# Windowed attention and a two-stage MoE layer on one core: a generator weave replaced by a planned program, with Q, K and x turned by DMA

## The chip, the core and the metric

The kernel runs on one core of a Trainium2 chip. The metric is the device time of one execution in microseconds. TensorE (PE) does the matmuls, with PEld its weight loads; VectorE (DVE), ScalarE (ACT) and GpSimd (POOL) do the elementwise work; SyncE (SP) issues transfers. PSUM holds what PE writes, and only DVE and ACT move it from there to SBUF.

## The reference

For 8 batches of 8 heads with 576 positions of 64 channels, attention over a causal window of 64 positions:

```python
scores = scale * np.matmul(q, k.transpose(0, 1, 3, 2))
mask = (rel >= 0) & (rel < window)          # rel = pos[:, None] - pos[None, :], window = 64
attn = softmax(np.where(mask, scores, -1e9))
attn_out = np.matmul(attn, v)
```

The heads of a position are joined to a row of 512, which gives x with 4608 rows, and then comes a layer with weights 512 x 2048 and 2048 x 512:

```python
h = x @ w_in
g = h * np.clip(h + 3.0, 0.0, 6.0) / 6.0
out = g @ w_out
```

All inputs and the output are float32.

## The kernel before

Matmuls take bf16 and add up in float32. The contraction runs over partitions, so Q, K and x are needed with channels on the partitions, and they arrive with positions there. Attention works on a pair of heads (group g, 4 per batch), since two heads of 64 channels fill 128 partitions; positions are cut into 5 blocks of 128.

The steps of a group, as generators in `attention` (line 170):

- `tq` (173): six PE transposes of Q (line 178) into a PSUM tile `tr`, copied to `QT` by DVE (187), then the same for K, copied by ACT (189). The casts to bf16 before it are `cast_batch` (149): DVE and ACT in batch 0, POOL later.
- `scores` (192): matmuls K x Q in two parts, key blocks 0 and 1, then 2, 3 and 4 (201); exp on ACT (208, 214); one multiply by the 0/1 mask on DVE (219).
- `pv` (224): 18 matmuls P x V (231, 236). V carries a column of ones, so the sum of a row comes along; reciprocal and product on DVE (242, 245) give `opg`.
- `xt` (251): five PE transposes (255), copied to `xT` by ACT (260).

The MoE layer works on blocks of 512 rows of x, 9 of them. `s1(T)` (273) makes 16 chunks of 128 hidden channels, each of 4 matmuls of 512 columns (280), a RELU on ACT (285) and a min-and-multiply on DVE (286). `s2(T)` (291) makes 4 tiles of 128 rows, each of 16 matmuls of 512 columns (296), a copy on ACT (303) and a store (305).

What sets the order is the program order of these generators. `zipped` (308) takes turns between a chunk of `s1(T)` and a quarter tile of `s2(T - 1)`, and `weave` (319) puts pieces of the next batch's attention between them by a fixed ratio. PSUM is given out by purpose: one `tr`, one `st`, one `o`, two `hT`, one `acc`.

Loads of a batch (`load_batch`, 67) are issued on SP: Q and K with six positions on each of 96 partitions (runs of 1536 B), V in five blocks with a position on each partition (runs of 256 B per head). There is one staging buffer per tensor, so the load of the batch after waits for the casts. The weights come by POOL's own queue with a cast on the way (94, 101).

Of the kernel before, what the change touches and what calls it, by code (L numbers as in the profile page):

```python
# [14 lines left out]
MIN = mybir.AluOpType.min  # L15
ISGE = mybir.AluOpType.is_ge
PSUM = bass.MemoryType.PSUM

WINDOW = 64


@with_exitstack
def kernel(
# [18 lines left out]
    R = 6  # L42
    NP = S // R
    NFC = FF // P
    TB = 512
    NTB = NT // TB
    assert NTB * TB == NT and NP * R == S
    QW = P + WINDOW
    VW = D + 1
    scale = 1.0 / math.sqrt(D)  # L50

    consts = ctx.enter_context(tc.tile_pool(name="consts", bufs=1))
    stage = ctx.enter_context(tc.tile_pool(name="stage", bufs=1))
    nat = ctx.enter_context(tc.tile_pool(name="nat", bufs=2))
    small = ctx.enter_context(tc.tile_pool(name="small", bufs=4))
    opool = ctx.enter_context(tc.tile_pool(name="opool", bufs=2))
    gpool = ctx.enter_context(tc.tile_pool(name="gT", bufs=2))
    t1pool = ctx.enter_context(tc.tile_pool(name="t1", bufs=3))
    osbp = ctx.enter_context(tc.tile_pool(name="osb", bufs=3))
    ps_tr = ctx.enter_context(tc.tile_pool(name="ps_tr", bufs=1, space=PSUM))  # L60
    ps_st = ctx.enter_context(tc.tile_pool(name="ps_st", bufs=1, space=PSUM))
    ps_o = ctx.enter_context(tc.tile_pool(name="ps_o", bufs=1, space=PSUM))
    ps_h = ctx.enter_context(tc.tile_pool(name="ps_h", bufs=2, space=PSUM))
    ps_acc = ctx.enter_context(tc.tile_pool(name="ps_acc", bufs=1, space=PSUM))


    def load_batch(b, by_pair):
        qst = stage.tile([P, H, R * D], F32, name="qst", tag="qst")
        kst = stage.tile([P, H, R * D], F32, name="kst", tag="kst")
        vst = stage.tile([P, KB, H, D], F32, name="vst", tag="vst")  # L70
        step = 2 if by_pair else H
        for h0 in range(0, H, step):
            for dst, src in ((qst, q), (kst, k)):
                nc.sync.dma_start(
                    out=dst[:NP, h0 : h0 + step, :],
                    in_=src[b, h0 : h0 + step].rearrange("h (p j) d -> p h (j d)", j=R),
                )
        for kb in range(KB):
            s0 = kb * P
            ss = min(P, S - s0)  # L80
            nc.sync.dma_start(  # L81
                out=vst[:ss, kb, :, :],
                in_=v[b, :, s0 : s0 + ss, :].rearrange("h s d -> s h d"),
            )
        return qst, kst, vst

    stage0 = load_batch(0, True)


    win16 = consts.tile([P, NG, FF], BF16, name="win16")  # L90
    wout16 = consts.tile([P, NFC, DM], BF16, name="wout16")
    WC = FF // 4
    for i in range(4):
        nc.gpsimd.dma_start(
            out=win16[:, :, i * WC : (i + 1) * WC],
            in_=moe_w_in[:, i * WC : (i + 1) * WC].rearrange("(g p) f -> p g f", p=P),
        )

    def load_w_out():
        for i in range(0, NFC, 4):  # L100
            nc.gpsimd.dma_start(
                out=wout16[:, i : i + 4, :],
                in_=moe_w_out[i * P : (i + 4) * P, :].rearrange("(c p) j -> p c j", p=P),
            )


    ident32 = consts.tile([P, P], F32, name="ident32")
    make_identity(nc, ident32)
    ident = consts.tile([P, P], BF16, name="ident")
    nc.vector.tensor_copy(out=ident[:], in_=ident32[:])  # L110
    mask32 = consts.tile([P, QW], F32, name="mask32")
    nc.gpsimd.memset(mask32[:], 1.0)
    nc.gpsimd.affine_select(
        out=mask32[:], in_=mask32[:], pattern=[[1, QW]], compare_op=ISGE,
        fill=0.0, base=0, channel_multiplier=-1,
    )
    nc.gpsimd.affine_select(
        out=mask32[:], in_=mask32[:], pattern=[[-1, QW]], compare_op=ISGE,
        fill=0.0, base=WINDOW - 1, channel_multiplier=1,
    )  # L120
    mask = consts.tile([P, 2 * KB, QW], BF16, name="mask")
    nc.vector.tensor_copy(
        out=mask[:], in_=mask32[:].unsqueeze(1).to_broadcast([P, 2 * KB, QW])
    )
    half = consts.tile([P, 1], F32, name="half")
    nc.vector.memset(half[:], 0.5)


    NQT, NPT, NV = 3, 3, 2
    QT_ring, KT_ring, P_ring, V_ring = [], [], [], []  # L130
    for i in range(NQT):
        for ring, n in ((QT_ring, "QT"), (KT_ring, "KT")):
            t = consts.tile([P, SP], BF16, name=f"{n}{i}")
            nc.vector.memset(t[:, S:SP], 0.0)
            ring.append(t)
    for i in range(NPT):
        t = consts.tile([P, 2, KB, 2 * P], BF16, name=f"pT{i}")
        nc.gpsimd.memset(t[:], 0.0)
        P_ring.append(t)
    for i in range(NV):  # L140
        t = consts.tile([P, KB, H, VW], BF16, name=f"V{i}")
        nc.gpsimd.memset(t[:, :, :, D:VW], 1.0)
        nc.gpsimd.memset(t[D:P, KB - 1, :, 0:D], 0.0)
        V_ring.append(t)

    xT = consts.tile([P, NG, NT], BF16, name="xT")


    def cast_batch(b, st, first):
        qst, kst, vst = st  # L150
        qn = nat.tile([P, R, H, D], BF16, name="qn")
        kn = nat.tile([P, R, H, D], BF16, name="kn")
        V = V_ring[b % NV]
        step = 2 if first else H
        for h0 in range(0, H, step):
            for i, (n, s) in enumerate(((qn, qst), (kn, kst))):
                o_ap = n[:NP, :, h0 : h0 + step, :].rearrange("p j h d -> p h j d")
                i_ap = s[:NP, h0 : h0 + step, :].rearrange("p h (j d) -> p h j d", j=R)
                if not first:
                    nc.gpsimd.tensor_copy(out=o_ap, in_=i_ap)  # L160
                elif i == 0:
                    nc.vector.tensor_copy(out=o_ap, in_=i_ap)
                else:
                    nc.scalar.copy(out=o_ap, in_=i_ap)
        nc.gpsimd.tensor_copy(out=V[:, 0 : KB - 1, :, 0:D], in_=vst[:, 0 : KB - 1, :, :])
        nc.gpsimd.tensor_copy(out=V[0:D, KB - 1, :, 0:D], in_=vst[0:D, KB - 1, :, :])
        return qn, kn, V


    def attention(b, cast):  # L170
        st8 = {}

        def tq(g):
            c = cast()
            for n, (src, ring) in enumerate(((c[0], QT_ring), (c[1], KT_ring))):
                tr = ps_tr.tile([P, 1024], BF16, name="tr")
                for j in range(R):
                    nc.tensor.transpose(  # L178
                        out=tr[:, j * NP : (j + 1) * NP],
                        in_=src[:NP, j, 2 * g : 2 * g + 2, :].rearrange("p h d -> p (h d)"),  # L180
                        identity=ident[:NP, :NP],
                    )
                T = ring[(b * NG + g) % NQT]
                o_ap = T[:, 0:S].rearrange("d (p j) -> d p j", j=R)
                i_ap = tr[:, 0:S].rearrange("d (j p) -> d p j", p=NP)
                if n == 0:
                    nc.vector.tensor_copy(out=o_ap, in_=i_ap)  # L187
                else:
                    nc.scalar.copy(out=o_ap, in_=i_ap)
                yield  # L190

        def scores(g):
            QT, KT = QT_ring[(b * NG + g) % NQT], KT_ring[(b * NG + g) % NQT]
            pT = P_ring[(b * NG + g) % NPT]
            for kbs in ((0, 1), (2, 3, 4)):
                st = ps_st.tile([P, 2, 512], F32, name="st")
                off = 0
                for kb in kbs:
                    w = min(QW, SP - kb * P)
                    for h in range(2):  # L200
                        nc.tensor.matmul(  # L201
                            st[:, h, off : off + w],
                            lhsT=KT[h * D : (h + 1) * D, kb * P : (kb + 1) * P],
                            rhs=QT[h * D : (h + 1) * D, kb * P : kb * P + w],
                            start=True, stop=True,
                        )
                    off += w
                nc.scalar.activation(  # L208
                    out=pT[:, :, kbs[0] : kbs[0] + 2, 0:QW],
                    in_=st[:, :, 0 : 2 * QW].rearrange("p h (k w) -> p h k w", k=2),  # L210
                    func=EXP, scale=scale,
                )
                if len(kbs) == 3:
                    nc.scalar.activation(  # L214
# [104 lines left out]
    def weave(main, n_main, side, n_side):  # L319
# [8 lines left out]
        for _ in main:  # L328
            pass
# [53 lines left out]
```

## Time and profile before

| what | value |
|---|---|
| median of 3 runs | 375.25 us (374.71 to 379.35) |
| span of the profiled execution | 372.6 us; its own device time is not given apart, the median lies 2.65 above the span |
| busy: PE, PEld | 333.0 us (89% of the span), 168.6 us (45%) |
| busy: ACT, DVE, POOL | 214.6 us (58%), 194.6 us (52%), 74.7 us (20%) |
| granted PE clock | 1.000 on the mean |
| read from and written to HBM | 36.70 MB, 9.44 MB |
| first-stage matmuls (280), 545 recorded | 152.2 us busy, mean 386 ns |
| second-stage matmuls (296), 559 recorded | 146.4 us busy, mean 379 ns |
| exp of 768 elements (208), output copy (303) | 0.81 us, 0.60 us each |
| V loads (81), store (305), issue to landing, median | 7.6 us, 2.0 us |

The page is of one profiled execution. Busy time of PE is a sum of matmul durations that overlap in the pipeline, so the cost of a matmul in a dense stretch is read from the distance between starts. The slices cut the span in 40 equal parts; a digit is the busy share in tenths, and the transfer row is the mean share of the 16 DMA engines. A few per cent of the matmul records are missing.

### The profile page before, as it was taken

How to read it: one execution, taken by the hardware profiler on the slowest of the kernel's cores; microseconds unless marked ns; L12 is line 12 of the kernel's file. 1: busy time of each engine (PE TensorE's matmuls, PEld its weight loads, DVE VectorE, ACT ScalarE, POOL GpSimd, SP SyncE). 2: the span in 40 equal slices, each digit the busy share in tenths (PEclk: the TensorE clock that was granted, in tenths of full speed). 3: DMA queues.
4: the chain of work that ended last, by engine and by line, in shares of the span. 5: the costliest groups of instructions: out<-in, count | busy, mean ns of one | idle time of the engine just before them, and what ended most of it. 6: DMA issues, size and time to landing. Idle time of an engine off the chain costs nothing.

```text
span 372.6 us, 6265 instructions
## 1 busy us (share of the span) xinstructions
PE 333.0 (89%) x2544; PEld 168.6 (45%) x2592; DVE 194.6 (52%) x285; ACT 214.6 (58%) x345; POOL 74.7 (20%) x54
## 2 busy tenths in 40 slices
PE   0156789999999999999999999999999999999985
PEld 0134434555545455455545554555445444444432
DVE  2444438865674567466746665656565643343300
ACT  2353358857666666766676667666766644544411
POOL 8505523544511051005200520000000000000000
PEclk9999999999999999999999999999999999999999
DMA  8999999999999148605760000000000010110111
GB/s 189 248 209 239 196 210 222 218 203 237 199 251 224 42 128 184 157 28 138 173 156 31 28 31 28 30 30 28 30 28 31 29 56 28 45 41 28 57 57 56
DMA packets 59676, 42.34 MB, mean 114 GB/s; under 512 B 38656, under 2 KB 55040, under 8 KB 59648
## 3 DMA queue, kind: packets, MB, share of 16 engines
q1 hardware_dynamic: 55424, 37.76, 43.2%
q0 software_dynamic: 4224, 4.19, 6.8%
q8 instruction: 20, 0.33, 0.4%
q14 instruction: 8, 0.07, 0.1%
HBM read 36.70 MB, written 9.44 MB: 124 GB/s over the span
## 4 chain that ended last, share of the span: by engine, by line
PE 51%; ACT 2%; DVE 2%; DMA 1%; another core or an unknown queue 1%; issue 1%; SPq 1%; ACTq 0%
PE acc L296 23%; PE hT L280 20%; PE st L201 2%; PE tr L178 2%; DMA vst<-in_v_dram 1%; PE o L231 1%; PE tr L255 1%; PE o L236 1%; ACT osb L303 1%; DVE pT_145 L219 1%; ACT pT_145 L208 0%; SPq L81 0%; DVE QT_131 L187 0%; DVE pT_147 L219 0%
## 5 line engine op out<-in xcount | busy, mean ns | idle before, releaser
L280 PE MATMUL hT<-xT,win_110 128*128 128x512 bf16 x545 | 152.2, 386 | 3.7 <-ACT xT L260 1.8
L296 PE MATMUL acc<-wout_111,gT 128*128 128x512 bf16 x559 | 146.4, 379 | 3.7 <-ACT osb L303 3.0
L280 PEld LDWEIGHTS <-win_110 128*128 128x128 bf16 x576 | 52.5, 99 | 58.2 <-issue 4.7
L296 PEld LDWEIGHTS <-gT 128*128 128x128 bf16 x576 | 50.6, 98 | 52.8 <-issue 6.3
L160 POOL CAST qn<-qst 96x3072 bf16<-96x3072 f32 x7 | 19.4, 2778 | 74.4 <-issue 56.9
L303 ACT COPY osb<-acc 128x512 f32<-128x512 f32 x36 | 21.6, 601 | 16.3 <-PE acc L296 12.6
L178 PE MATMUL tr<-ident,qn 96*128 96x96 bf16 x192 | 14.9, 219 | 16.7 <-DVE ident L110 15.8
L245 DVE TENSOR_TENSOR opg<-o,rec 128x640 bf16<-128x640 f32 x32 | 26.4, 825 | 1.1
L260 ACT COPY xT<-tr 128x576 bf16<-128x576 bf16 x32 | 20.6, 642 | 9.0 <-PE tr L255 8.5
L178 PEld LDWEIGHTS <-qn 96*128 96x128 bf16 x192 | 12.8, 105 | 25.2 <-issue 14.0
L208 ACT ACTIVATE pT_147<-st 128x768 bf16<-128x768 f32 x20 | 16.1, 808 | 11.5 <-PE st L201 11.5
L208 ACT ACTIVATE pT_143<-st 128x768 bf16<-128x768 f32 x22 | 17.8, 808 | 7.1 <-PE st L201 7.1
L208 ACT ACTIVATE pT_145<-st 128x768 bf16<-128x768 f32 x22 | 17.7, 806 | 5.5 <-PE st L201 5.5
L160 POOL CAST kn<-kst 96x3072 bf16<-96x3072 f32 x7 | 19.2, 2740 | 6.6 <-DMA kst<-in_k_dram 6.6
L219 DVE TENSOR_TENSOR pT_143<-pT_143,mask 128x1920 bf16<-128x1920 bf16 x11 | 13.2, 1199 | 9.8 <-ACT pT_143 L214 9.8
L219 DVE TENSOR_TENSOR pT_145<-pT_145,mask 128x1920 bf16<-128x1920 bf16 x11 | 13.2, 1196 | 9.5 <-ACT pT_145 L214 9.5
L178 PEld LDWEIGHTS <-kn 96*128 96x128 bf16 x192 | 12.8, 105 | 11.1 <-issue 5.9
L178 PE MATMUL tr<-ident,kn 96*128 96x96 bf16 x192 | 14.8, 219 | 3.0 <-DVE QT_135 L187 1.3
L255 PE MATMUL tr<-ident,opg 128*128 128x128 bf16 x160 | 15.5, 231 | 2.0 <-DVE opg L245 1.2
L219 DVE TENSOR_TENSOR pT_147<-pT_147,mask 128x1920 bf16<-128x1920 bf16 x10 | 12.5, 1253 | 8.5 <-ACT pT_147 L214 8.5
L255 PEld LDWEIGHTS <-opg 128*128 128x128 bf16 x160 | 11.4, 102 | 10.6 <-DVE opg L245 4.4
L242 DVE RECIPROCAL rec<-o 128x10 f32<-128x10 f32 x32 | 6.9, 217 | 10.6 <-PE o L236 10.6
(355 smaller groups left out, 429.7 us busy)
## 6 DMA issues: line engine op xcount, KB each, us to landing
out_dram<-osb SPq DMA_DIRECT2D x36, 256.0 KB, 2.0
vst<-in_v_dram SPq DMA_DIRECT2D x32, 256.0 KB, 7.6
qst<-in_q_dram SPq DMA_DIRECT2D x6, 1152.0 KB, 9.2
kst<-in_k_dram SPq DMA_DIRECT2D x6, 1152.0 KB, 12.8
qst<-in_q_dram SPq DMA_DIRECT2D x8, 288.0 KB, 7.7
kst<-in_k_dram SPq DMA_DIRECT2D x8, 288.0 KB, 8.5
win_110<-in_moe_w_in_dram POOLq DMA_DIRECT2D x4, 512.0 KB, 15.2
wout_111<-in_moe_w_out_dram POOLq DMA_DIRECT2D x4, 512.0 KB, 15.0
```

The costliest lines, as they stand in the source:

```text
L160: nc.gpsimd.tensor_copy(out=o_ap, in_=i_ap)
L178: nc.tensor.transpose(out=tr[:, j * NP : (j + 1) * NP], in_=src[:NP, j, 2 * g : 2 * g + 2, :].rearrange("p h d -> p (h d)"), identity=iden ...
L201: nc.tensor.matmul(st[:, h, off : off + w], lhsT=KT[h * D : (h + 1) * D, kb * P : (kb + 1) * P], rhs=QT[h * D : (h + 1) * D, kb * P : kb * ...
L208: nc.scalar.activation(out=pT[:, :, kbs[0] : kbs[0] + 2, 0:QW], in_=st[:, :, 0 : 2 * QW].rearrange("p h (k w) -> p h k w", k=2), func=EXP, ...
L219: nc.vector.tensor_tensor(out=pT[:, :, :, 0:QW], in0=pT[:, :, :, 0:QW], in1=mask[:].rearrange("p (h k) w -> p h k w", h=2), op=MULT,)
L242: nc.vector.reciprocal(out=rec[:].unsqueeze(3), in_=ov[:, :, :, D:VW])
L245: nc.vector.tensor_tensor(out=opg[:].rearrange("p k h d -> p h k d"), in0=ov[:, :, :, 0:D], in1=rec[:].unsqueeze(3).to_broadcast([P, 2, KB ...
L255: nc.tensor.transpose(out=tr[:, qb * P : (qb + 1) * P], in_=opg[:, qb, :, :].rearrange("p h d -> p (h d)"), identity=ident[:],)
L260: nc.scalar.copy(out=xT[:, g, b * S : (b + 1) * S], in_=tr[:, 0:S])
L280: nc.tensor.matmul(hT[:], lhsT=win16[:, g, fc * P : (fc + 1) * P], rhs=xT[:, g, t0 : t0 + TB], start=(g == 0), stop=(g == NG - 1),)
L296: nc.tensor.matmul(acc[:], lhsT=gT[:, fc, ts * P : (ts + 1) * P], rhs=wout16[:, fc, :], start=(fc == 0), stop=(fc == NFC - 1),)
L303: nc.scalar.copy(out=osb[:], in_=acc[:])
```

## The change

The whole body is written anew. Every operation is now entered in a plan (`Plan.add`) with its engine, a duration that the author supplies, what it reads and writes, and a stream. `Plan.solve` walks through the plan, each time picking the operation with the smallest start less its stream's rank, and the instructions are issued engine by engine in the order of the planned starts. PE and SP each have streams that stay in order within themselves.

What else is different:

- PSUM is four slots of two banks, given out by the plan to any purpose.
- MoE runs per batch of 576 rows. The first stage makes a chunk from 8 matmuls of 288 columns (two halves in two banks of a slot), one RELU and one multiply of 576. It runs dense: attention of the next batch is held back by a gate until the last chunk's matmuls. Attention is then woven with the second stage, which has 4 tiles in even batches and 5 in odd ones; the 64 rows that an even batch leaves over are kept by a copy on POOL (`keep_left`).
- Batches 0 and 1: Q and K arrive as one load per pair of heads, with 9 positions on a partition, are cast into the two diagonal halves of a zeroed tile `A`, and are turned on PE by 9 matmuls of 64 columns against a folded identity (`fold_pair`).
- From batch 2 on Q and K are loaded like V (a position on a partition, runs of 256 B), cast by POOL, and turned by one DMA transpose each for the whole batch (`turn`, 20 blocks of 128 x 128). There is one `T` buffer each for Q and K.
- x of batch 0 is turned on PE, of every later batch by one DMA transpose per group (`xt_dma`, 5 blocks).
- Weights are loaded on SP as float32 into staging buffers and cast by POOL, after the loads of batch 0 and before those of batch 1. Six staging buffers are used in turn, three per batch.
- The mask is one block of 192 broadcast over blocks, and its multiply is split in two like the exps. The exps of the last key block cover 64 query columns, not 128.

All transfers, transposes included, are issued on SP. The core of the diff, mostly new lines:

```diff
+class Plan:
+    LAT = 150
+    NSLOT = 4
...
+    def solve(self, rank, rate, dma_lat):
...
+        inorder = {k for k in streams if k[0] in ("PE", "SP")}
...
+                    if eng == "SP":
+                        t = max(t, lanes[nlane % 8])
+                    k = (t - rank.get((eng, op.stream), 0) - op.prio, t, op.seq)
...
+            if op.eng == "SP":
+                free["SP"] = t + op.dur
+                begin = max(t + dma_lat, dma_free)
+                dma_free = begin + op.nbytes / rate
+                op.done = dma_free + 500
...
+        order.sort(key=lambda o: (o.start, o.seq))
+        return order
...
+    slots = [psum.tile([P, 2, 512], F32, name=f"ps{i}") for i in range(4)]
...
+    T = {n: sb([P, NG, SP], BF16, f"T{n}") for n in "qk"}
...
+    def load_tok(src, b, i, g0, g1):
...
+            dma(250 + 40 * (g1 - g0), ss * (g1 - g0) * P * 4 * 1.6, st[:ss, kb, hs, :],
+                src[b, hs, s0 : s0 + ss, :].rearrange("h s d -> s h d"),
...
+    def turn(n, b, g0, g1):
+        dma(300, (g1 - g0) * P * SP * 2 * 1.6,
+            T[n][:, g0:g1, :].rearrange("d g (k s) -> d (g k) s", k=KB),
+            qn[n][:, g0:g1, :, :].rearrange("p g k c -> p (g k c)"),
+            reads=[("n", n, g) for g in range(g0, g1)], writes=[("T", n, g) for g in range(g0, g1)],
+            stream="turn", kind="turn")
...
+    def fold_pair(n, b, g, eng, gate):
...
+            for j in range(R):
+                nc.tensor.matmul(sl[:, j * D : (j + 1) * D], lhsT=a[:, j, :, :].rearrange("p h d -> p (h d)"),
+                                 rhs=fold[:], start=True, stop=True)
...
+    def xt_dma(b, g):
+        j = (b * NG + g) % NOPG
+        dma(200, P * SP * 2 * 1.6, xT[b % 2][:, g, :].rearrange("d (k s) -> d k s", k=KB),
+            opg[j][:].rearrange("p k h d -> p (k h d)"),
+            reads=[("opg", j)], writes=[("xT", b % 2, g)], stream="xt", kind="turn")
...
+    def s1(b, fc):
...
+            for g in range(NG):
+                for hf in range(2):
+                    nc.tensor.matmul(hp[:, hf, 0:HS], lhsT=win16[:, g, fc * P : (fc + 1) * P],
+                                     rhs=x[:, g, hf * HS : (hf + 1) * HS], start=(g == 0), stop=(g == NG - 1))
...
+    def s2(b, u, col, idx, ntile):
+        name = ("ACC", b)
+        bank = idx % 2
...
+                for fc in range(4 * c, 4 * c + 4):
+                    nc.tensor.matmul(acc, lhsT=gT[:, fc, col : col + P], rhs=wout16[:, fc, :],
+                                     start=(fc == 0), stop=(fc == NFC - 1))
...
+    def attend_rows(b, st, gate):
+        iq, ik, iv = st
+        cast_tok("q", b, iq, 0, NG)
+        cast_tok("k", b, ik, 0, NG)
+        turn("q", b, 0, NG)
+        turn("k", b, 0, NG)
+        cast_v(b, iv, 0, NG)
+        pend = []
+        for g in range(NG):
+            pend.append(scores(b, g, gate))
+            if g:
+                pv(b, g - 1, pend[g - 1], gate)
+                xt_dma(b, g - 1)
+        pv(b, NG - 1, pend[NG - 1], gate)
+        xt_dma(b, NG - 1)
+
+    st0 = load_fold(0)
+    attend_fold(0, st0, (), (("DVE", "DVE"), ("ACT", "POOL")))
+    for i in range(4):
+        load_win(i)
+    for i in range(4):
+        load_wout(i)
+    stq = load_fold(1)
+    u = 0
+    for b in range(B):
+        last = None
         for fc in range(NFC):
...
+            last = s1(b, fc)
+        if b % 2 == 0:
+            keep_left()
+        if b + 1 < B:
+            if b == 0:
+                attend_fold(1, stq, (last,), (("POOL", "POOL"), ("POOL", "POOL")))
+            else:
+                attend_rows(b + 1, stq, (last,))
+            if b + 2 < B:
+                stq = load_rows(b + 2)
+        ntile = KB - 1 if b % 2 == 0 else KB
+        col = LEFT if b % 2 == 0 else 0
+        for t in range(ntile):
+            s2(b, u, col + t * P, t, ntile)
+            u += 1
...
+    rank = {("PE", "att"): 300, ("SP", "xt"): 2000, ("SP", "turn"): 1000, ("SP", "st"): 500}
+    order = pl.solve(rank, 360.0, 1300)
+    with tc.manual_schedule():
+        for op in order:
+            op.emit()
```

In the built program the order on SP around batch 3's x turns, for example, is: x turn of group 0, a load, x turn of group 1, the turns of Q and K of batch 4, x turn of group 2, two stores, x turn of group 3; before these stand the loads up to most of batch 6. The batches' order on PE in a woven stretch is: scores of groups 0 and 1, 12 matmuls of the second stage, PV of group 0, scores of group 2, and so on, with what is left of the second stage after PV of group 3.

## The prediction, made before the changed kernel ran

> **What bounds the kernel now.** I read the 40 slices first, then the chain, then the groups, then the instructions of one batch in order of time, last the transfers.
>
> ```profile
> PE   0156789999999999999999999999999999999985
> PEclk9999999999999999999999999999999999999999
> DMA  8999999999999148605760000000000010110111
> GB/s 189 248 209 239 196 210 222 218 203 237 199 251 224 42 128 184 157 28 138 173 156 31 28 31 28 30 30 28 30 28 31 29 56 28 45 41 28 57 57 56
> ```
>
> A slice is 9.3 us. PE fills up over the first six slices while the transfers are saturated, and is then full to the end at full clock; after slice 20 the transfers carry little but the output. So there are two costs: a start of some 50 us, and a body paced by matmuls. The chain agrees (51% on PE), and its masks mark the body's period:
>
> ```profile
> 158.57 1.16 DVE pT_145 L219
> ...
> 195.35 1.16 DVE pT_147 L219
> ...
> 232.14 1.16 DVE pT_143 L219
> ```
>
> 36.78 us per batch. What fills it, from the order of time:
>
> ```profile
> 192.31 0.34 PE L201 MATMUL st<-QT_139,KT_141 64*128 64x192 bf16 x4
> ...
> 192.58 1.04 PE L280 MATMUL hT<-xT,win_110 128*128 128x512 bf16 x4
> ...
> 195.62 0.42 PE L178 MATMUL tr<-ident,qn 96*128 96x96 bf16 x6
> ...
> 195.88 1.03 PE L296 MATMUL acc<-wout_111,gT 128*128 128x512 bf16 x4
> ...
> 203.04 0.44 PE L255 MATMUL tr<-ident,opg 128*128 128x128 bf16 x5
> ```
>
> Starts count, not durations, which overlap. Four MoE matmuls take 0.864 us in the dense end (301.58 to 302.45), 216 ns each. Six Q or K transposes: 195.62 to 195.88, 0.26 us, 43 ns each. Five x transposes at 128 columns: 0.28 by the same line. Scores of a pair: 0.27 (192.31 to 192.58) and 0.33 for the six of the second part, 0.60. The 18 matmuls of P times V: 198.13 to 198.68, 0.55, 31 ns each at 65 columns. Sum: 128 x 0.216 + 8 x 0.26 + 4 x 0.28 + 4 x (0.60 + 0.55) = 35.4 of 36.78; only 1.3 us of a period is waiting. The old weave wastes little.
>
> Transfers, in windows of 0.5 us and 1 us and by queue:
>
> ```profile
> 154.00:154.50 0.50, 1.00 1.19 269
> 154.50:155.00 0.50, 1.00 1.11 252
> 155.00:155.50 0.50, 1.00 0.98 205
> ```
>
> ```profile
> 32.00:33.00 1.00, 1.00 1.07 240
> ```
>
> ```profile
> q1 hardware_dynamic: 55424, 37.76, 43.2%
> q0 software_dynamic: 4224, 4.19, 6.8%
> ```
>
> The last column is GB/s. V alone, in runs of 256 B, is saturated from 153.5 to 157: seven windows, mean 228. Q and K in 1536 B runs hold 240. The weights (q0, 2 KB rows, 8.39 MB read) cost 6.8% of 372.6, 25.3 us. One output store costs 0.7 us (0.07 of a 10 us window with one store).
>
> **The change, part by part.** *PE work.* Removed: all transposes of seven batches and Q/K of batch 0, 8 x 3.2 = 25.6 us less the 1.1 of x in batch 0. Added: 144 fold matmuls in batches 0 and 1 at 31 ns (65-column row), 4.5 us. The first stage is now 1024 matmuls of 288 columns: between 31 ns at 65 and 216 at 512 that is 123 ns, 126.0 us against 124.4. Second stage: the same 576, 124.4. With scores and PV 8 x 4.6 = 36.8 the floor is 292.8 us against 248.8 + 8 x 7.8 = 311.2 now: 18.4 less. If nothing else moved, 354.
>
> *ACT, DVE and POOL.* Stage one asks per 0.98 us of PE for one RELU and one multiply of 576; the rows of 512 take 0.69 and 0.68, so about 0.77 each. Matmul, RELU, multiply and hand-overs make 2.8 us of a slot; four slots cover 3.9. Hidden by PE; if the cover went, 0.1 us x 128. The split masks cost the same elements. POOL's memsets (2.23 us each) now stand ahead of its first K cast, so attention 0 starts near 14.5 instead of 4; it ends near 33, and the first stage of batch 0 near 49. This is covered by the transfer stream below.
>
> *The first dense batch.* SP is one queue and its order is fixed. Ahead of the last x turn of batch 1, which stage one of batch 1 waits for, stand: Q/K of batches 0 and 1 (4.72 MB, taken at 240 GB/s) 19.7; their V (2.36 MB at 228) 10.3; weights 25.3; Q, K and four fifths of V of batch 2 in 256 B runs, 10.3 + 4.6; two Q/K turns, four x turns, three stores 2.1; start and landing 3.
>
> A turn has no row. It moves 256 B rows, 20 blocks of 32 KB (0.655 MB) for Q or K and 5 (0.164 MB) for x. From below, it costs as little per byte as a store (0.26 MB in 0.7: 374 GB/s); from above, as V's median landing in a full queue, 256 KB in 7.6 us, 34 GB/s. I take V's 228, the row with the same run length: 2.9 and 0.72 us, 8.6 per batch. The sum is 19.7 + 10.3 + 25.3 + 14.9 + 8.6 + 2.1 + 3 = 84 us. PE has nothing else from about 66 to 84: this stall is the price of the new order (the old kernel is dense from 50).
>
> [...]
>
> *The rest.* From 84: seven first stages 7 x 15.75 = 110.3; 32 tiles of the second at 3.456 = 110.6; six attentions at 4.6 = 27.6; together 248.5. The end after the last matmul is 3.6 (369.0 to 372.6 now).
>
> *Waits in a woven stretch.* Stage two of a batch (13.8 us with four tiles, 17.3 with five) and the next attention share PE in fixed order. The first PV needs exps (0.81 each on ACT, after the last RELUs) and its split mask: near 4.9 us after stage one, while PE arrives at 3.8. I put 1.1 us per stretch, six stretches 6.6; between 0 and 4. The Q/K turns of the batch after wait for the last scores (one Tq, one Tk buffer), and two x turns and the stores are queued behind them on SP: issued near 8.9, all landed near 18.2, PE needs them at 19.5 (23 with five tiles). Covered, by 1.3 us.
>
> *Stream ahead of PE.* Loads run two batches ahead on the same rings. Up to the x turns of batch 3 the stream carries 13.0 MB (56.9), two batches of turns (17.2), nine stores (6.3): 84 + 81 = 165, and PE wants them at 84 + 38.7 + 35.3 = 158: 7 us stall. For batch 4 it needs 33 more, PE 39: none.
>
> Sum: 84 + 248.5 + 3.6 + 6.6 + 7 = 349.7 us of span, against 372.6. The median of the runs, 375.25, lies 2.65 above that span; so 352.
>
> **Rivals.** *Turns too slow (the other side).* Stores and loads up to the x turns of batch 4 need 162 us, four batches of turns 4 x 1.97 MB / r, and from there 63 + 62.2 + 13.8 + 3.3 + 3.6 = 145.9 of PE work remain: 308 + 7864/r us. The stream decides below r = 188 GB/s; at 121 the gain is gone; at 100 it is 387, at the upper bound of 34 it is 539. For: a turn is scattered on the write side, and no row shows that. Against: its read side is V's run length.
>
> *Turns late, not slow (about no change).* If each ends 4 us later than counted, the margin of 1.3 is gone and each of six stretches loses about 3: 18 more, 370. For: the shortest load landing is 2.8 us, and each x turn is on PE's path. Against: five-tile stretches have 3.5 us more.
>
> *Reads faster.* With both queues running the windows from 9 to 16 us hold about 270 GB/s; if 256 B runs get that, stage one of batch 1 starts at 77 and the 7 us lag goes: 336 span, 338. For: the weights get 331. Against: V alone never held 270 for 2 us.
>
> *That it doesn't do what it says:* PE's transposes are gone for certain; only if the stall returns them is there no change, which is the case above.
>
> **How the numbers follow.** Forecast 0.57 (own range 341 to 364), reads faster 0.09, late turns 0.15, slow turns 0.19. Faster by over 2% (below 367.7; 2% is about what a measurement of this kernel tells from no change): 0.57 + 0.09 + a third of the late turns, 0.71. Within 2%: the other two thirds and 0.02 of the slow, 0.12. Slower: 0.17. The range 336 to 390 leaves out the slow turns below about 96 GB/s (0.13) and a few hundredths under it.
>
> **What would show it.** PE idle between about 66 and 84 us, then full in seven repetitions of a dense 15.7 us; 288-column matmuls 123 ns apart; x turns landing within 3 us of issue once loads are over; turns of 0.66 MB in 3 us; transfers saturated to about 200 us. I am wrong if PE waits for x at every stage one after 200 us (late or slow turns), if stage one is paced by ACT or DVE, or if it starts for batch 1 far from 84.

## The result, and the profile after

The changed kernel takes 378.4 us (median of 20 runs, 376.8 to 381.4), against 375.1 us of the kernel before beside it (20 runs): a ratio of 1.012, with a 95% interval of 1.009 to 1.014. Ratios leave out executions that lie more than 1.5% above the fastest of their kernel, eight of the 20 of the kernel before; the medians alone would give 1.009. So it is about 1% slower, where the forecast had 6% faster. The profiled execution took 378.4 us with a span of 376.7, 27 us above the span of the forecast.

The same rows of the page as were shown of before; a slice is now 9.42 us:

```profile
PE   0335899885979979992999999998999899999985
PEclk9999999996999999997799999999999999999999
DMA  8999995789999999999999950087008700330021
GB/s 221 311 390 387 290 199 88 161 183 201 216 207 217 182 245 232 208 186 221 238 205 153 162 156 2 0 138 185 2 2 163 159 28 2 82 101 3 1 79 62
```

Three things differ from the picture that the forecast drew. PE is not idle from 66 to 84 us (digits 8 and 8); its holes are later, at 85 to 94 and at 170 to 179 us. The clock row, all nines before, falls to 6 and 7 in the slices of these holes. And the transfers, which were to be saturated to about 200 us, have a gap in the seventh slice (88 GB/s), after slices of 390: the loads ran ahead and then stood still.

What PE waited for (releaser, us in total, times, longest):

```profile
PE ps L507 <- DMA xT<-opg: 17.8, 7, 5.9
PE ps L543 <- ACT osb L549: 8.6, 13, 0.7
PE ps L361 <- POOL Ak L306: 6.8, 1, 6.8
PE ps L361 <- DVE Aq L302: 6.2, 1, 6.2
...
PE ps L442 <- DVE pT L422: 4.5, 3, 3.0
```

L507 is stage one, L543 stage two, L361 the folds of batch 0, L442 PV. The kernel before has the counterparts of the first two, but small:

```profile
PE acc L296 <- ACT osb L303: 3.0, 4, 0.9
PE hT L280 <- ACT xT L260: 1.8, 2, 1.1
```

**The wait for x** can be followed through batch 1, engine by engine in order of time (start, duration). First DVE finishing the products of groups 2 and 3, then the queue on SP, then PE:

```profile
76.40 0.82 DVE L455 TENSOR_TENSOR opg<-ps,rec 128x640 bf16<-128x640 f32 x1
...
79.54 0.82 DVE L455 TENSOR_TENSOR opg<-ps,rec 128x640 bf16<-128x640 f32 x1
```

```profile
75.94 3.09 SPq L275 DMA_TRANSPOSE Tq<-nq  x1
79.09 0.56 SPq L273 DMA_DIRECT2D stage<-in_v_dram  x1
79.76 1.25 SPq L275 DMA_TRANSPOSE xT<-opg  x1
81.07 0.57 SPq L273 DMA_DIRECT2D stage<-in_v_dram  x1
81.73 0.53 SPq L273 DMA_DIRECT2D out_dram<-osb  x1
82.35 3.80 SPq L275 DMA_TRANSPOSE Tk<-nk  x1
86.25 1.23 SPq L275 DMA_TRANSPOSE xT<-opg  x1
```

```profile
88.91 6.27 PE L507 MATMUL ps<-xT,win 128*128 128x288 bf16 x37 [5.35 <-DMA xT<-opg]
```

Six of the 128 matmuls of this stage one run from 81.95 on, with the x of groups 0 to 2; the dense run starts at 88.91. The product of group 3 is ready at 80.36. Its turn is issued at 86.25, because the turn of K, whose own result is not needed before the end of the coming stage one, holds SP for 3.80 us in front of it, and a load and a store stand there too. The turn itself is quick: 88.91 less 86.25 is 2.66 us. Issue to landing over the whole run (us, median) shows the same:

```profile
xT<-opg SPq DMA_TRANSPOSE x28, 2.7
...
Tq<-nq SPq DMA_TRANSPOSE x6, 5.1
Tk<-nk SPq DMA_TRANSPOSE x6, 5.0
```

At batch 1 SP had nothing left over from earlier: it stood still from 73.3 to 75.94, until the last scores, which read the buffer that Q's turn writes, were done (75.46). At batches 2 and 3 loads come on top. Before the x turns of batch 3 SP issues loads and two stores without a gap from 135.2 us on; the product of group 0 is ready at 156.28, and its turn goes out at 164.03:

```profile
153.65 5.67 SPq L273 DMA_DIRECT2D stage<-in_q_dram  x5
159.41 4.52 SPq L273 DMA_DIRECT2D stage<-in_k_dram  x4
164.03 1.77 SPq L275 DMA_TRANSPOSE xT<-opg  x1
...
167.97 3.05 SPq L275 DMA_TRANSPOSE Tq<-nq  x1
...
176.73 1.25 SPq L275 DMA_TRANSPOSE xT<-opg  x1
```

**The clock.** Windows of 2 us (busy us of PE, PEld, DVE, ACT, POOL with counts; granted clock; transfer share; GB/s):

```profile
84.00:86.00 2.00, 0.00 (x0) 0.00 (x0) 0.00 (x0) 0.00 (x0) 1.58 (x1) 0.83 1.17 241
86.00:88.00 2.00, 0.00 (x0) 0.00 (x0) 0.00 (x0) 0.00 (x0) 0.31 (x1) 0.50 1.05 192
...
90.00:92.00 2.00, 2.00 (x11) 1.19 (x9) 0.75 (x1) 0.82 (x2) 0.61 (x1) 0.50 0.84 208
92.00:94.00 2.00, 2.00 (x17) 1.58 (x16) 1.10 (x2) 1.12 (x3) 0.00 (x0) 0.96 1.04 231
...
182.00:184.00 2.00, 2.00 (x10) 1.25 (x9) 0.76 (x1) 0.74 (x1) 0.00 (x0) 0.50 1.21 281
```

In the wait at batch 1 the clock falls to 0.50, and it stays there for some 3 us after work is back (88.91 to about 92). At batch 3 it is low from 174 to 184. In both stretches the matmuls of stage one start 240 ns apart, and 121 to 124 ns right behind them, so this work is half lost: half of 3.2 us in the first place, half of some 5.4 busy us in the second, about 4.3 together. The wait of 2.25 us at batch 2 leaves the clock at 1.00.

**The tile boundary.** A tile of stage two is 16 matmuls; between two tiles of one batch PE stands still:

```profile
288.93 3.61 PE L543 MATMUL ps<-wout,gT 128*128 128x512 bf16 x16
293.22 3.61 PE L543 MATMUL ps<-wout,gT 128*128 128x512 bf16 x16 [0.67 <-ACT osb L549]
```

The two tiles use different banks, but of one slot, which is declared as one PSUM tile; the second waits 0.67 us for the copy out of the first.

From the start of stage one of batch 1 to the last matmul the forecast had 262.1 us, and it took 284. Of the 22 us more, waits for x are 4.9 (11.9 after that start, where 7 were put), tile boundaries 8.2, half clock 4.3; the other 4.6 are what remains, and lie for the most part in the woven stretches. The start itself is 4.9 late.

### The profile page after: what moved, and what is told of

It reads as the page before. It is cut to its first block, busy times and chain, and to the rows that moved or that the text cites. A ratio compares the mean times of both kernels' runs of the same rounds, so it can differ in the third digit from the quotient of the medians.

```text
span 376.7 us, 6641 instructions
## 1 busy us (share of the span) xinstructions
PE 311.8 (83%) x2660; PEld 199.3 (53%) x2660; DVE 193.8 (51%) x280; ACT 178.7 (47%) x277; POOL 97.6 (26%) x99
## 4 chain that ended last, share of the span: by engine, by line
PE 66%; DVE 9%; ACT 9%; SPq 6%; POOL 3%; DMA 3%; issue 2%; ACTq 0%; POOLq 0%
PE ps L507 32%; PE ps L543 27%; DVE pT L422 6%; SPq L275 5%; ACT osb L549 4%; ACT pT L402 4%; DMA xT<-opg 3%; PE ps L394 3%; POOL pT L240 2%; PE ps L442 2%; DVE gT L518 1%; ACT t L513 1%; PE ps L445 1%; DVE opg L455 1%; SPq L273 1%
## 5 line engine op out<-in xcount | busy, mean ns | idle before, releaser
L518 DVE SCALAR_TENSOR_TENSOR gT<-t,ps 128x576 bf16<-128x576 bf16 x128 | 96.6, 754 | 116.4 <-ACT t L513 116.4
L507 PE MATMUL ps<-xT,win 128*128 128x288 bf16 x1024 | 133.4, 294 | 17.8 <-DMA xT<-opg 17.8
L543 PE MATMUL ps<-wout,gT 128*128 128x512 bf16 x576 | 134.1, 380 | 10.3 <-ACT osb L549 8.6
L507 PEld LDWEIGHTS <-win 128*128 128x128 bf16 x1024 | 102.3, 100 | 48.9 <-issue 19.3
L513 ACT ACTIVATE t<-ps,half 128x576 bf16<-128x576 f32 x128 | 94.8, 740 | 45.9 <-PE ps L507 45.9
L543 PEld LDWEIGHTS <-gT 128*128 128x128 bf16 x576 | 53.8, 97 | 73.1 <-issue 15.0
L402 ACT ACTIVATE pT<-ps 128x768 bf16<-128x768 f32 x64 | 49.4, 816 | 21.9 <-PE ps L394 21.3
L422 DVE TENSOR_TENSOR pT<-pT,mask 128x768 bf16<-128x768 bf16 (+1 forms) x64 | 51.0, 826 | 6.1 <-ACT pT L402 5.4
L442 PEld LDWEIGHTS <-pT 128*128 128x128 bf16 x320 | 21.8, 101 | 12.9 <-DVE pT L422 5.9
L442 PE MATMUL ps<-V,pT 128*128 128x65 bf16 x320 | 23.9, 200 | 5.2 <-DVE pT L422 4.5
L455 DVE TENSOR_TENSOR opg<-ps,rec 128x640 bf16<-128x640 f32 x32 | 26.4, 825 | 1.3 <-DVE rec L454 0.2
L445 PE MATMUL ps<-V,pT 128*128 128x65 bf16 x256 | 22.8, 200 | 0.0
L394 PEld LDWEIGHTS <-Tk 64*128 64x128 bf16 x320 | 12.9, 98 | 17.4 <-issue 12.3
L331 POOL CAST nq<-stage 128x2048 bf16<-128x2048 f32 x6 | 11.4, 1892 | 31.0 <-DMA Tq<-nq 17.6
L445 PEld LDWEIGHTS <-pT 128*128 128x128 bf16 x256 | 19.3, 102 | 0.0
L361 PE MATMUL ps<-fold,Ak 128*128 128x64 bf16 x72 | 4.4, 218 | 6.8 <-POOL Ak L306 6.8
```

Of the source, the lines that this page charges most:

```text
L331: nc.gpsimd.tensor_copy(out=qn[n][:, gs, 0 : KB - 1, :], in_=st[:, gs, 0 : KB - 1, :])
L394: nc.tensor.matmul(sl[:, h, off : off + w], lhsT=T["k"][r, g, kb * P : (kb + 1) * P], rhs=T["q"][r, g, kb * P : kb * P + w], start=True, s ...
L402: nc.scalar.activation(out=p_[:, :, k0 : k0 + 2, 0:QW], in_=slots[op.slot][:, :, 0 : 2 * QW].rearrange("p h (k w) -> p h k w", k=2), func= ...
L422: nc.vector.tensor_tensor(out=ap, in0=ap, in1=mask[:].unsqueeze(1).unsqueeze(1).to_broadcast([P, 2, nkb, QW]), op=MULT,)
L442: nc.tensor.matmul(ob, lhsT=p_[:, h, qb, 0:P], rhs=v16[:, qb, 2 * g + h, :], start=True, stop=(qb == 0))
L445: nc.tensor.matmul(ob, lhsT=p_[:, h, qb - 1, P : 2 * P], rhs=v16[:, qb - 1, 2 * g + h, :], start=False, stop=True)
```

## The experiments

The theory after reading the trace: the sum of the forecast was the time of this program without two hold-ups, the order on SP in front of the x turns, and the tile boundary of stage two. The rivals: the turns or the stream of loads are late whatever the order, or the waits are only moved. The first four runs take the hold-ups away, one by one and together. Each time is a median; ratios are to the kernel before, measured beside it.

**Turns of Q and K after the x turns.**

```diff
-        turn("q", b, 0, NG)
-        turn("k", b, 0, NG)
+        turn("q", b, 0, NG, after=(xlast[b - 1],))
+        turn("k", b, 0, NG, after=(xlast[b - 1],))
```

> One edit to the changed kernel: the DMA turns of Q and K of a batch are held in SP's order until the last x turn of the batch before. Theory (order on SP): the last x turn of a batch was issued 5.8 us after its product (80.4 to 86.25 in batch 1) because the turns of Q and K (3.09 and 3.80 us of issue) and loads stood ahead of it. So stage one of batch 1 starts near 83.5 and not 88.9, the waits for x at the later batches fall from 11.4 us to 5 or less, and some of the half-clock stretches (86 to 92 and 174 to 184 us, about 4.5 us of lost matmul work) go with them: device time 362 to 370, against 378.4. Rival (the turns themselves land late, or the rings are full): the last x turn is issued early but lands as late as before; gain under 4 us, 374 to 379. Second rival (loads ahead of x): only the start of batch 1 gains, 5 us: 372 to 374.

Measured: 363.6 us, ratio 0.970 (0.964 to 0.976). PE's waits for x fall from 17.8 to 4.9 us (3 times, longest 2.0), stage one of batch 1 starts at 83.1, the granted clock is 0.995 on the mean where it was 0.976. The theory's range; the rival of slow landings falls, since nothing but the place in the queue was changed.

**Loads held.** `xlast[b - 2]` is the last x turn of two batches before.

```diff
-        load_tok(q, b, iq, 0, NG)
+        load_tok(q, b, iq, 0, NG, after=(xlast[b - 2],))
...
```

> One edit to the changed kernel: the loads of a batch are held in SP's order until the last x turn of two batches before, so no load stands ahead of x turns whose products are ready; the turns of Q and K stay ahead of the last x turns. Theory (order on SP, loads): the waits of 2.9 us at batch 2 and 7.8 us at batch 3 fall to about 1 each and the half clock at 174 to 184 us goes; batch 1 still starts near 88.9: device time 366 to 372. Rival (Q and K turns are what is in the way): waits stay within 3 us of what they were: 375 to 379. Other side: the held loads make the casts and turns of Q and K late, and PE waits for scores: over 380.

Measured: 369.2 us, ratio 0.981 (0.971 to 0.991). What is left of the wait for x is almost all at batch 1:

```profile
91.40 16.46 PE L510 MATMUL ps<-xT,win 128*128 128x288 bf16 x122 [5.48 <-DMA xT<-opg]
```

So loads, too, stood in front of x turns, at batches 2 and 3; at batch 1 it was the turns of Q and K. At the same time PE's waits for masks grow from 4.5 to 10.0 us, which takes back a part of the gain.

**A slot for each tile of stage two.**

```diff
-        name = ("ACC", b)
-        bank = idx % 2
+        name = ("ACC", b, idx)
+        bank = 0
...
-        if idx == ntile - 1:
-            e.frees = (name,)
+        e.frees = (name,)
```

> One edit to the changed kernel: each tile of the second stage takes a PSUM slot of its own (first bank) and gives it back after its copy, where the changed kernel kept one slot per batch and alternated its two banks. Theory (a tile's first matmul waits for the copy of the tile before because both lie in one PSUM tile): the 12 waits of 0.7 us, 8.2 us in all, go; up to half may come back as waits for slots: device time 370 to 374 against 378.4. Rival (the wait is only moved): PE waits the same sum for free slots or for x, 376.5 to 379; if a tile now takes a slot from the scores, up to 382.

Measured: 366.3 us, ratio 0.975 (0.967 to 0.982). PE has no wait for an output copy left. The gain of about 12 us is more than the 8.6 of the waits that it takes away, and above the expected range. The slot now also comes free between tiles, which could help the scores; that part was not taken apart.

**All three.**

> The three edits together (turns of Q and K after the last x turn, loads held, one slot per tile of the second stage). Theory (the forecast failed by SP's order and by the tile boundaries): stage one of batch 1 starts near 83.5, then 248.5 us of PE work, some 9 us of waits in the woven stretches, 3.6 at the end and 1.7 around the span: 343 to 354. Rival (x lands late whatever its place, or the stream is full): PE still waits for x at most of the stages one, 362 to 372.

Measured: 351.0 us, ratio 0.937 (0.931 to 0.944): the forecast's 352 within its own scatter. On SP the last x turn now goes out ahead of the turns of Q and K, and stage one follows at once:

```profile
83.06 1.25 SPq L275 DMA_TRANSPOSE xT<-opg  x1
86.06 0.36 SPq L273 DMA_DIRECT2D out_dram<-osb  x1
86.52 4.26 SPq L275 DMA_TRANSPOSE Tq<-nq  x1
90.88 3.15 SPq L275 DMA_TRANSPOSE Tk<-nk  x1
```

```profile
85.20 7.02 PE L510 MATMUL ps<-xT,win 128*128 128x288 bf16 x56
```

and tiles of stage two run on without a break, 47 matmuls in 10.31 us:

```profile
267.11 10.31 PE L546 MATMUL ps<-wout,gT 128*128 128x512 bf16 x47
```

There is no wait for x left. The three single gains (15, 9 and 12 us) sum to 36, the joint one is 27: the first two edits take away parts of the same waits (12.9 and 10.5 us of waits for x alone, of 17.8 that there were). The other 3 us of the difference were not taken apart.

The next four start from this version. **x turned on PE:**

```diff
-            (xt_pe if b == 0 else xt_dma)(b, g - 1)
+            xt_pe(b, g - 1)
...
```

> From the version with all three edits (351.0 us): x of every batch is turned on PE with an ACT copy, as batch 0's is; Q and K stay with the transfers. Theory (with the order on SP mended, turning x by transfer saves what PE paid): 28 groups at 0.28 us are 7.8 us more on PE and nothing waits less: 357 to 363. Rival (PE has gaps in the woven stretch that take the transposes for nothing, or the landing of an x turn costs as much): 349 to 354.

Measured: 350.0 us, ratio 0.935 (0.931 to 0.939): no difference. The theory falls; of the 7.8 us that 140 transposes more cost PE, 1.2 show between the start of stage one of batch 1 and the last matmul (261.7 us against 260.5), and the rest fits into waits of the woven stretch.

**Q and K folded on PE in all batches:**

```diff
-                attend_rows(b + 1, stq, (last,))
+            attend_fold(b + 1, stq, (last,), (("POOL", "POOL"), ("POOL", "POOL")))
...
-                stq = load_rows(b + 2)
+                stq = load_fold(b + 2, (xlast[b],))
```

> From the version with all three edits (351.0 us): Q and K of every batch are turned by folded matmuls on PE, as in batches 0 and 1, and loaded as there in long runs; x stays with the transfers. Theory (the DMA turns save PE time): six batches at 72 matmuls of 31 ns are 13.4 us more on PE, and the copies out of PSUM (0.75 us on DVE, 0.64 on ACT, four each per batch) stand in the woven stretch: 362 to 372. Rival (loads in 256 B runs and the turns cost as much elsewhere, as the waits for masks beside POOL's casts): 349 to 357.

Measured: 354.5 us, ratio 0.947 (0.945 to 0.949), 3.5 us slower, not 13. But stage one of batch 1 starts 5.0 us earlier here (80.2 against 85.2 us), and from there to the last matmul it takes 7.6 us more (268.1 against 260.5): more than half of the 13.4. Both outcomes still say that the woven stretch was not paced by PE alone.

**Attention in both stages.**

```diff
-                attend_rows(b + 1, stq, (last,))
+                attend_rows(b + 1, stq, ())
...
```

> From the version with all three edits (351.0 us): the gate that keeps attention out of the first stage is taken away, and the planner may put the next batch's attention into both stages (it now looks 96 operations ahead on each engine, not 24, since it found no order otherwise). Theory (PE is the bound, dense or woven makes no difference): 347 to 355. Rival (attention's masks and products meet the 0.75 us multiplies of stage one on DVE, which is busy 77 % of that stage): PE waits for free slots, 356 to 366.

Measured: 363.4 us, ratio 0.971 (0.967 to 0.975). The time is the rival's, its reason is not. PE's longest wait is now this one:

```profile
PE ps L396 <- DMA Tk<-nk: 10.5, 6, 3.1
```

With the turns of Q and K sent after the x turns, scores that move into stage one come too early for them. So this run does not tell whether a dense stage is better by itself; that stays open.

**The start on ACT.** In the version before this edit POOL reaches its first K cast only after its memsets, and PE waits (POOL, then PE):

```profile
12.98 1.27 POOL L306 CAST Ak<-stage 64x576 bf16<-64x576 f32 x2
```

```profile
13.70 0.66 PE L363 MATMUL ps<-fold,Ak 128*128 128x64 bf16 x9 [6.79 <-POOL Ak L306]
```

```diff
-    attend_fold(0, st0, (), (("DVE", "DVE"), ("ACT", "POOL")))
+    attend_fold(0, st0, (), (("DVE", "DVE"), ("ACT", "ACT")))
```

> From the version with all three edits (351.0 us): in batch 0 the second half of each K cast is given to ACT instead of POOL, which is busy with its memsets until 12.98 us. Theory (attention 0 sets the start of everything up to stage one of batch 1, since the transfers ran ahead): stage one of batch 0 starts 4 to 6 us earlier than 41.8, that of batch 1 as much earlier than 85.2: 345 to 348. Rival (the forecast's step: the stream of transfers sets the first dense batch, attention 0 is covered): stage one of batch 0 earlier, that of batch 1 not: 349.5 to 352.5.

Measured: 341.1 us, ratio 0.912 (0.909 to 0.915). Stage one of batch 0 starts at 33.6 instead of 41.8, that of batch 1 at 73.3 instead of 85.2, with the same bytes on the same queue:

```profile
33.62 17.01 PE L510 MATMUL ps<-xT,win 128*128 128x288 bf16 x128
73.27 0.90 PE L510 MATMUL ps<-xT,win 128*128 128x288 bf16 x6
```

The forecast's step, that the stream sets the first dense batch and attention 0 is covered by it, falls. The gain of 10 us is above the theory's, which had 4 to 6 us at the start: attention 0 now also meets fewer of POOL's weight casts, and two of its eight masks take over 1 us (1.36 and 1.06) where five took 1.48 to 2.24. Why 8 us at batch 0 became 12 at batch 1 was not taken apart.

**x on PE alone.** Back to the changed kernel, with only x turned on PE and everything else as it was:

> From the changed kernel (378.4 us), one part undone: x of every batch is turned on PE; everything else as in the changed kernel, the order on SP included. Theory (what was lost to x is only the place of its turns on SP): the 17.3 us of waits for x and the half clock after them (about 4.5 us) go, and the transposes fit into gaps as in the run before: 356 to 363. Rival (loads and turns of Q and K are late as well, x was only the first to show it): PE waits for T or V in its place, over 368.

Measured: 356.5 us, ratio 0.941 (0.930 to 0.952). No wait for x beyond 0.2 us, clock 1.000 on the mean:

```profile
PE ps L507 <- ACT xT L485: 0.2, 1, 0.2
```

The loads still keep the transfers at digits of 8 and 9 in all but one of the slices up to 195 us, and PE does not feel it: the stream was never late, only the x turns in it were.

**POOL's casts held.** The version with the start on ACT has one more odd line. A mask that takes 0.56 us in one place takes 2.17 in another, and POOL casts beside it (DVE, then POOL):

```profile
171.88 2.17 DVE L424 TENSOR_TENSOR pT<-pT,mask 128x768 bf16<-128x768 bf16 x1
```

```profile
171.75 1.90 POOL L316 CAST V<-stage 128x2048 bf16<-128x2048 f32 x1 [2.80 <-DMA stage<-in_v_dram]
173.59 0.94 POOL L319 CAST V<-stage 64x512 bf16<-64x512 f32 x1
```

```diff
-        cast_tok("q", b, iq, 0, NG)
+        cast_tok("q", b, iq, 0, NG, after=(xlast[b - 1],))
...
```

> From the version with the three edits and the start on ACT (341.1 us): POOL's casts of Q, K and V of a batch from batch 2 on are held until the last x turn of the batch before, so that they run beside the dense first stage and not beside the masks of the woven stretch. Theory (a mask of 768 elements takes 0.56 us alone and 2 to 2.8 us beside a cast, and PE waits for it): no mask above 1 us in the stretches from batch 3 on, five-tile periods fall from 40.4 to about 38.8 us: 336 to 339. Rival (the slow masks are covered by the second stage): 340 to 342. Other side (the turns of Q and K, now issued later, make the first scores wait): over 343.

Measured: 348.5 us in the profiled execution and 353.8 to 354.9 in the three others, so at least 7 us slower; the ratio is not settled. The edit missed its aim. The hold exists in the plan only: POOL casts Q of batch 3 from 85.42 us on, and the last x turn of batch 2 leaves at 107.66. On the chip POOL kept nothing but its order, and there the casts of every other batch now stood behind `keep_left`, right in the woven stretch (DVE, then POOL):

```profile
132.02 5.84 DVE L424 TENSOR_TENSOR pT<-pT,mask 128x768 bf16<-128x768 bf16 x3 [0.84 <-ACT pT L404]
```

```profile
132.02 2.30 POOL L331 CAST nq<-stage 128x2048 bf16<-128x2048 f32 x1
...
135.36 1.89 POOL L331 CAST nk<-stage 128x2048 bf16<-128x2048 f32 x1
```

Three masks take 5.84 us, another three 8.24, and these two four-tile periods take 39.5 and 41.1 us instead of 35.3 and 36.0. That is 9.3 us, about what the span of this execution is longer by (346.8 against 338.0 us). So the run shows, the other way round, that masks beside casts cost the path time.

**No transfer turns at all,** with the start on ACT:

> From the version with the three edits and the start on ACT (341.1 us): no transfer turns anything; Q and K of all batches are folded on PE, x of all batches is turned on PE. Theory (from the two runs that undid one of them each, plus 3.5 and minus 1 us: the woven stretch has room on PE): 342 to 347. Rival (the forecast's floor: 13.4 and 7.8 us of PE work come back in full once both are there): 355 to 363.

Measured: 349.0 us, ratio 0.925 (0.918 to 0.932): 7.9 us above the version that turns by transfer, a little over the theory's range, and far under the 21 of the rival. Stage one of batch 1 starts at 73.1 here and 73.3 there, so the difference lies behind it. This is what the DMA turns of the change are worth here; the masks are a little quicker without them (at most 1.23 us against 2.45), which is in the number.

**K's and V's casts on ACT,** behind the exps of the batch before (`nlast`: the product of its last PV), with the start on ACT:

```diff
-        cast_tok("k", b, ik, 0, NG)
+        cast_tok("k", b, ik, 0, NG, "ACT", (nlast[b - 1],))
...
-        cast_v(b, iv, 0, NG)
+        cast_v(b, iv, 0, NG, "ACT", (nlast[b - 1],))
```

> From the version with the three edits and the start on ACT (341.1 us): K's and V's casts of a batch from batch 2 on go from POOL to ACT and stand there behind the exps of the batch before, in the last third of the woven stretch, where ACT has only output copies (the planner looks 40 operations ahead). Theory (masks of 0.56 us take 2 to 2.8 us beside a POOL cast and PE waits for them): masks stay under 1 us, five-tile periods fall from about 40.4 to 38.8 us and the four-tile ones by up to half a microsecond: 335 to 339. Rival (slow masks are covered, the waits of the woven stretch come from exps and slots): 340 to 342. Other side (2.5 us casts on ACT hold up output copies, RELUs of the next stage or the turn of K): 343 to 350.

Measured: 335.6 us, ratio 0.898 (0.896 to 0.900), the fastest here and better than both kernels. Three masks of a stretch again, as in the run before last, now 1.90 us and not 5.84; then stage one of two batches in a row:

```profile
167.75 1.90 DVE L430 TENSOR_TENSOR pT<-pT,mask 128x768 bf16<-128x768 bf16 x3 [0.84 <-ACT pT L410]
```

```profile
187.77 15.84 PE L517 MATMUL ps<-xT,win 128*128 128x288 bf16 x128
223.09 15.84 PE L517 MATMUL ps<-xT,win 128*128 128x288 bf16 x128
```

After 66 us no mask takes longer than 0.75 us. A four-tile period is 35.32 us, a five-tile one (223.09 to 261.87) 38.78. The forecast had 35.3 and 38.75. The planner's look-ahead was raised from 24 to 40 with this edit, and no run separates the two; that the slow masks are gone and the periods shorter is what the theory of the casts expects.

## Why the prediction was wrong

*PE floor and the woven stretch: right in size.* Matmuls of 288 columns are 123 ns apart, a first stage takes 15.84 us (15.75 forecast), RELU and multiply 0.740 and 0.754 us (0.77) are hidden by PE. With the hold-ups gone and the masks quick (the last run), the periods from batch 2 on equal the forecast to 0.03 us, its wait of 1.1 us per stretch included. In the changed kernel itself that wait was too small, for the tile boundary and the slow masks were not in it. Both could have been read: the wait of a tile for the copy before it stood among the waits of the kernel before (3.0 us, 4 times, the weave hid the rest), and the listing plans casts of POOL beside masks.

*"Covered, by 1.3 us": the step that failed.* The forecast let the turns of Q and K go first and counted them by their transfer time: issued 8.9 us after the end of stage one, with all x landed 9.3 us later. It left out that SP is occupied while it issues. A turn holds it for 3.03 to 3.80 us for Q or K (the forecast's 2.9 of transfer was about right in size) and 1.20 to 2.77 for x (0.72), a load or a store for 0.5 to 1.0, by the median of each tensor. From the issue of Q's turn to the landing of the last x turn it took 11.6 to 13.0 us at batches 2 to 6, not 9.3. And at batches 2 and 3 loads stood in front, so that Q's turn left 17.6 and 18.0 us after stage one; once the last load is out (200.9 us) it leaves 9.6 to 10.7 after it, and PE waits for x only once more, 1.2 us. At batch 1 there was no backlog; there the last x turn left 5.9 us after its product, behind K's turn, where 1.3 were to spare. "I am wrong if PE waits for x" was the right thing to look for, and the rival "turns late, not slow" (370 us, given 0.15) was the mechanism; with the half clock and the boundaries on top it came to 378.

*Stream ahead of PE: wrong cause.* A 7 us lag by volume was put at batch 3. There PE did wait 5.9 us at one stroke (7.8 in all), but for the place of the x turns in the order: with x off SP the loads run on nearly full to 195 us and PE has no such wait.

*The first dense batch: near in number, wrong in reason.* 84 us was the sum of all bytes. The weights were costed at the 331 GB/s of their old queue and came in slices at up to 390, so the stream got ahead and then stopped. What set the start was attention 0. The forecast had its start behind POOL's memsets right (near 14.5; the first scores are at 15.1) and called it covered. Its end was too early, 41.6 us and not 33: five of its eight masks ran beside POOL's weight casts and took 1.49 to 2.24 us. Eight microseconds gained there were 12 at batch 1.

*The agreement of 351.0 with 352 is thus partly luck.* In that version stage one of batch 1 starts at 85.2 (84), the six periods take 227.4 us (222.1 and the 7 of lag), the time from the last stage one to the end 36.8 (36.6). The first is right by another cause, and in the second the slow masks stand where the lag was put.

*Half clock: not in the sum.* In the kernel before the clock is 1.00 from 55.7 us to the last matmul, and the forecast let a wait cost its length. In the changed kernel the clock fell to 0.50 in the waits of 5.35 and 5.92 us and stayed there for some 3 us of work at batch 1, and about 4 after 180 us, where the work is steady again; after the wait of 2.25 us at batch 2 it was 1.00. What length of wait brings it down was not shown.

*Turned by transfer or on PE.* The forecast booked 24.5 us of removed transposes, 18.4 net of what PE gets in their place, as the gain. The runs put the worth of all DMA turns at 7.9 us, and that of x alone at nothing within the scatter (350.0 and 351.0). What a turn costs the forecast took from the loads of V, 2.9 us for Q or K; a Q turn of 20 blocks occupies SP for 3.09 us, 155 ns a block, and has landed after 5.1. x kept on PE, with the rest as it was, does avoid the loss (356.5).

What stays open: whether a dense first stage is better than a woven one, what the extra gain of the separate slots is, how much of the last run's gain is the planner's longer look-ahead, and the worth of the turns once masks are quick.

## What to carry to other kernels

An in-order queue is a resource with a path of its own: for each transfer that the bound engine waits for, list what is issued in front of it and for how long each occupies the issuer (here 3.80 us for one turn of K), and put what is needed latest last. Read from the listing what is declared as one tile (8.6 us of waits here), and which elementwise work runs beside the casts of another engine (here a mask of 0.75 us took 3.0). Before a saving on the bound engine is booked in full, ask whether the stretch that it leaves was full: work taken from a stretch with waits is worth only what is left after these (here 350.0 us with x turned on PE, 351.0 by transfer).

## What the hardware showed that was not expected

- DVE's mask multiply (two operands in SBUF) takes 0.55 to 0.56 us (768 elements) or 0.74 to 0.76 (1152) wherever no POOL instruction overlaps it in the changed kernel. Beside POOL's casts it takes up to 3.0 us there, and up to 5.4 in the run with held casts; beside POOL's copy of the left rows it stays at 0.56. The product of stage one, which reads PSUM and one SBUF operand, keeps to 746 to 756 ns in all 128 instances of the changed kernel, 16 of them beside casts. What makes the two differ no run separates.
- A DMA turn of 5 blocks occupies SP for 1.20 to 2.77 us in the changed kernel (median 1.23), one of 20 blocks for 3.03 to 3.80 (4.26 once in the version with all three edits), where the loads and stores among them from 79 to 89 us take 0.53 to 0.66 and loads in a row 1.1 each (five in 5.46). What makes some of them longer no run separates.
- Loads of 2 KB rows on SP reach 390 GB/s over a slice of 9.4 us; while loads in rows of 256 B and turns fill the transfers, the slices hold 153 to 245.
- After the waits of 5.35 and 5.92 us in the changed kernel PE's granted clock is 0.50, for about 3 and 4 us of work; after the one of 2.25 us it is 1.00. Profiled executions in which PE waits for no x and no turn longer than 2.0 us have 0.995 to 1.000 on the mean.
- The clock row does not show the start. The trace of the changed kernel has no clock record before 44.4 us, and its views print 1.00 there; but the stage-one matmuls start 240 ns apart from 41.4 us on and 121 to 124 from 44.5 on, so stage one of batch 0 takes 17.30 us and not 15.84. In the kernel before the record begins at 55.7 us, and matmuls that follow each other directly start 423 to 427 ns apart at 51 to 54 us and 215 to 217 from 55.8 on. Both begin at half rate.
